# Where three weight chunks of the first expert are loaded: the later chunks' pool in place of the first chunks' buffers

## The chip, the core and the metric

The kernel runs on one core of one Trainium2 chip, in one launch. The metric is the device time of a run in microseconds. Every time below is of the kernel before the change.

## What is computed

Three stages follow each other. Sliding-window attention with sink tokens (2 batches, 8 heads, 768 positions, head width 64) gives 1536 rows of 512. A gated product follows, and then a mixture of eight experts: each token goes to one expert, in the order of the gate's logits over all tokens and experts, at most 192 tokens to an expert.

```python
x = attention(q, k, v, n_sink, window)          # (1536, 512)
x = (x @ w_a * (x @ w_b)) @ w_out               # w_a, w_b: 512 x 1536
logits = x @ w_gate                             # 8 experts
# greedy assignment in descending order of all logits, 192 tokens an expert
for e in range(8):
    out[mask[e]] = np.maximum(x[mask[e]] @ w1[e], 0.0) @ w2[e]   # 512 x 1024, 1024 x 512
```

## The kernel before, in words

All large products are made from split operands: a float32 operand is cut into a high part (`ehi`, `gh`, `woh`, ...) that TensorE (PE) takes at full rate and a low part (`elo`, `gl`, `wol`, ...) with the rest, and three products of the parts are added in PSUM.

*The second product and the routing* (`run`, from line 712). `second` computes x in twelve blocks of 128 tokens, 36 matmuls each (line 977). The routing's steps are woven into it by `fill`, so that PE has matmuls while DVE and ACT rank the logits. At the end of a block ACT copies it from PSUM (line 983), and ACT's DMA queue writes it to the tensor `x2d` in HBM (line 984). The last block, of 128 tokens, is also kept on the chip as `x2last`.

*The first expert's rows* (`first_rows`, line 1009). When the routing has given the tokens of each expert (`idx`), two indirect DMAs of POOL (GpSimd) gather the first expert's rows from the first eleven blocks of `x2d` into `first0` (128 rows) and `first1` (64 rows), line 1018. They have to wait until the eleventh block is written. Rows of the twelfth block don't come from HBM: a matmul with a 0/1 matrix picks them from `x2last` (line 1147). The gathered rows are turned by 16 matmuls with the identity (`begin_rows`, line 1035), eight for each gather.

*The weights of the experts.* Each expert has eight chunks of 512 KB, four of w1 and four of w2, so chunk c belongs to expert c // 8. `weight_load` (line 987) issues one DMA per chunk from SP's queue (line 997), into a buffer named `eraw`. ACT makes `ehi` from it (line 1002) and DVE `elo` (line 1007); then the buffer is free. Two pools hold `eraw`: `exraw` with three buffers (line 703), opened when the second product begins, and `more` with six buffers (line 1044), opened with the experts. Chunks 0 to 3 go to `exraw`, long before they are wanted; they are converted at the end of the routing (lines 738 to 743). SP's queue works strictly in order: a load whose buffer is not free holds up the loads behind it.

`more` lies in memory that the second product's operands and `x2` hold until then, so its first load waits for PE, ACT, POOL and the writes of x2d to be done with them.

*The experts* (`experts`, line 1038). PE, ACT and DVE work in the order in which the lines are written. For each expert, four steps make the hidden values (`product1`, line 1092; ACT's `part`, DVE's `h`, ACT's `hT`), then four steps make the output (`product2`, lines 1098 to 1103). In each step `high` converts chunks for later steps: the list CONV = (5, 6, 6, 7, 9, 10, 11, 12) says how many chunks of this expert and the next have to be converted by each of the eight steps. The conversion of chunk 4 stands in the first step, between `part` and `hT`. `load` (line 1072) is called for four chunks from the one being converted; SP runs ahead of this as far as free buffers let it. At the end of an expert's second step of outputs, the next expert's gathered rows (`xe`, line 1051) are turned.

Of the kernel before, what the change touches and what calls it, by code (L numbers as in the profile page):

```python
# [67 lines left out]
class Kernel:  # L68
# [969 lines left out]
    def experts(self, tag, exraw, trp, first=None, weights=None):  # L1038
# [4 lines left out]
        scat, xe, xt, raws, ready = [], {}, {}, {}, {}  # L1043
        with tc.tile_pool(name="ex" + tag, bufs=2) as pool, tc.tile_pool(name="er" + tag, bufs=EXR2) as more, \
# [26 lines left out]

            def load(c):
                if c < 8 * E and c not in raws and c not in ready:
                    raws[c] = self.weight_load(exraw if weights and c < 7 else more, c)

            def high(s):

                while pend:
                    self.weight_low(ready[pend.pop(0)])
                for c in range(8 * (s // 8) + CONV[s % 8]):  # L1080
                    if c < 8 * E and c not in ready:
                        for n in range(c, c + 1 + EARLY):
                            load(n)
                        ready[c] = self.weight_high(pool, raws.pop(c), EB)
                        pend.append(c)
# [47 lines left out]
            for c in range(4, 4 + EARLY):  # L1133
                load(c)
# [201 lines left out]
```

## Time and profile before

| | |
|---|---|
| Median of three runs | 646.68 us (645.85, 646.68, 648.88) |
| The profiled execution | 648.35 us, of which the span from the first to the last instruction is 646.1 us |
| PE busy | 620.3 us, 96% of the span |
| DVE, ACT, POOL busy | 404.0, 337.3 and 175.9 us (63%, 52%, 27%) |
| Mean granted clock of PE | 0.976 of full speed |
| DMA | 72.16 MB, 112 GB/s over the span |

The page divides the span into 40 slices of 16.2 us. PE is busy for 90% or more in nearly all of them, and the granted clock is below 90% in three: the first, the last, and the one from 468 to 485 us, where the second product has ended and the first expert begins. This is the place that the diff touches. In the rows below, times are microseconds from the start of the span; an entry "[7.54 <-DMA first]" says how long the engine was idle before the instruction and what ended that. Which event ended a wait is inferred from the times of the semaphore events, so of two events that fall together the wrong one can be named. PEld is the loading of weights into PE; an engine's name with a q behind it is its queue of instructions.

### The profile page before, as it was taken

Reading aid. Unit: us, or ns where it says so; the run is one execution under the profiler, and the core shown is the slowest. Engines: PE = TensorE matmul, PEld = TensorE weight load, DVE = VectorE, ACT = ScalarE, POOL = GpSimd, SP = SyncE. Lnnn points to the kernel's source line nnn. Section 1 sums busy time; section 2 is a strip of 40 time slices with the busy share of each in tenths; the row PEclk is TensorE's granted clock in tenths of the full one; section 3 lists DMA queues with packets and bytes.
Section 4 is the critical chain, followed back from the end, with each engine's and each line's share of the span. In section 5 each row is a group of like instructions: output and inputs, shape, how many; then the busy total and the mean of one; then the engine's idle time right before and its main releaser. Section 6 shows DMA issues by size and latency. Waiting matters only on the chain.

```text
span 646.1 us, 10265 instructions
## 1 busy us (share of the span) xinstructions
PE 620.3 (96%) x3705; PEld 491.2 (76%) x3705; DVE 404.0 (63%) x873; ACT 337.3 (52%) x669; POOL 175.9 (27%) x299
## 2 busy tenths in 40 slices
PE   7999999999999999999999999999869999999994
PEld 5767777778878888788866776677668888888883
DVE  5788876579966767342126556666207787777782
ACT  3788777644442334122126655663307666668671
POOL 5557664400000000001024344344321222232221
PEclk7999999999999999999999999999959999999997
DMA  7966310044542233200040000000381888787841
GB/s 161 219 123 159 66 67 2 2 129 133 164 130 77 88 98 98 66 0 1 0 131 17 18 33 17 34 17 33 119 281 26 276 253 260 257 245 231 259 144 34
DMA packets 82602, 72.16 MB, mean 112 GB/s; under 512 B 41072, under 2 KB 69744, under 8 KB 82544
## 3 DMA queue, kind: packets, MB, share of 16 engines
q1 hardware_dynamic: 78704, 61.99, 33.3%
q0 software_dynamic: 2112, 6.30, 3.0%
q10 hardware_dynamic: 1728, 3.15, 1.3%
q8 instruction: 31, 0.51, 0.3%
q14 instruction: 27, 0.22, 0.1%
HBM read 65.13 MB, written 6.29 MB: 111 GB/s over the span
## 4 chain that ended last, share of the span: by engine, by line
PE 80%; issue 9%; DVE 3%; DMA 2%; POOL 2%; ACT 1%; POOLq 0%; DVEq 0%; ACTq 0%
PE pa L559 14%; PE pb L559 14%; PE px L977 13%; PE p L1092 7%; PE pa L470 4%; PE s L273 4%; PE px L367 4%; PE pa L334 3%; POOL out_dram L1107 2%; PE pq L856 2%; PE pw L662 1%; PE pt L237 1%; DVE gt L845 1%; PE y L1098 1%; PE y L1099 1%
## 5 line engine op out<-in xcount | busy, mean ns | idle before, releaser
L1007 DVE TENSOR_TENSOR elo<-eraw,ehi 128x1024 fp32r<-128x1024 f32 x64 | 75.9, 1216 | 5.0 <-ACT ehi L1002 5.0
L1092 PE MATMUL p<-xt,ehi 128*128 128x384 f32 x256 | 73.6, 360 | 0.0
L963 POOL TENSOR_TENSOR gl<-G,gh 128x512 fp32r<-128x512 f32 (+1 forms) x40 | 47.9, 1206 | 71.5 <-ACT gh L962 71.5
L1002 ACT ACTIVATE ehi<-eraw 128x1024 fp32r<-128x1024 f32 x64 | 65.0, 1054 | 3.8 <-DVE oidx L932 2.3
L1092 PE MATMUL p<-xt,elo 128*128 128x192 f32 x256 | 64.7, 254 | 0.0
L977 PE MATMUL px<-woh,gh 128*128 128x512 f32 x144 | 59.9, 416 | 0.0
L279 ACT ACTIVATE A<-sm,negmax 128x264 f32<-128x264 f32 (+1 forms) x96 | 46.9, 490 | 23.6 <-DVE negmax L277 22.5
L963 POOL TENSOR_TENSOR gl<-GE,gh 128x256 fp32r<-128x256 f32 x8 | 7.1, 882 | 188.4 <-ACT gh L962 184.9
L845 DVE TENSOR_SCALAR gt<-lgT,vmax 128x1536 bf16<-128x1536 f32 x40 | 45.4, 1196 | 20.4 <-ACT lgT L820 17.7
L977 PE MATMUL px<-woh,gl 128*128 128x512 f32 x144 | 57.6, 400 | 0.0
L977 PE MATMUL px<-wol,gh 128*128 128x512 f32 x144 | 57.5, 399 | 0.0
L566 DVE TENSOR_TENSOR G<-asb,pb 128x512 f32<-128x512 f32 x32 | 21.9, 685 | 54.7 <-PE pb L559 54.7
L301 POOL TENSOR_SCALAR A<-A,rs 128x256 f32<-128x256 f32 (+1 forms) x96 | 43.2, 469 | 44.8 <-DVE rs L288 24.9
L559 PE MATMUL pb<-xh,whi 128*128 128x512 f32 x128 | 51.1, 399 | 0.0
L559 PE MATMUL pa<-xh,whi 128*128 128x512 f32 x128 | 50.9, 398 | 0.0
L1107 POOL DMA_INDIRECT out_dram<-o,oidx x16 | 26.3, 1645 | 90.2 <-ACT o L1116 68.2
L559 PE MATMUL pb<-xh,wlo 128*128 128x512 f32 x128 | 50.1, 391 | 0.0
L559 PE MATMUL pb<-xl,whi 128*128 128x512 f32 x128 | 50.0, 390 | 0.0
L559 PE MATMUL pa<-xh,wlo 128*128 128x512 f32 x128 | 49.9, 390 | 0.0
L1092 PEld LDWEIGHTS p<-xt,elo 128*128 128x128 f32 x256 | 49.4, 193 | 0.6 <-ACT xt L1069 0.2
L559 PE MATMUL pa<-xl,whi 128*128 128x512 f32 x128 | 49.8, 389 | 0.0
L1092 PEld LDWEIGHTS p<-xt,ehi 128*128 128x128 f32 x256 | 48.3, 189 | 0.7
(220 smaller groups left out, 1439.5 us busy)
## 6 DMA issues: line engine op xcount, KB each, us to landing
eraw<-in_moe_w_dram SPq DMA_DIRECT2D x64, 512.0 KB
wraw<-in_moe_w_a_dram SPq DMA_DIRECT2D x12, 512.0 KB
wraw<-in_moe_w_b_dram SPq DMA_DIRECT2D x12, 512.0 KB
wraw<-in_moe_w_out_dram SPq DMA_DIRECT2D x12, 512.0 KB
x2d<-x ACTq DMA_DIRECT2D x11, 256.0 KB
rawv<-in_v_dram SPq DMA_DIRECT2D x10, 256.0 KB
rawq<-in_q_dram SPq DMA_DIRECT2D x8, 256.0 KB
rawk<-in_k_dram SPq DMA_DIRECT2D x8, 256.0 KB
```

Source lines behind the costliest of these rows:

```text
L273: nc.tensor.matmul(s[:, :n], T[hs, tq, 6 + i % 2, 0:128], flat[hs, tk, lo:lo + n], start=(t == 0), stop=(t == 2))
L279: nc.scalar.activation(st.A2[:, j, h, c0:], sm[:, :n], AF.Exp, bias=self.negmax[:, cc], scale=-1.0, accum_out=self.sums[:, cc])
L301: nc.gpsimd.tensor_scalar(blocks, blocks, st.r2[:, j, h:h + 1], 1.0, op0=OP.mult, op1=OP.mult)
L367: nc.tensor.matmul(px[64 * h:64 * h + 64, cols], vv[:, vcol[h]], st.AT[h][:, sl].rearrange("p a b -> p (a b)"), start=(not g and n == 0), ...
L559: nc.tensor.matmul(pab[m], w[:, k, :], x[:, k, :], start=(k == 0 and t == 0), stop=(k == 3 and t == 2))
L845: nc.vector.tensor_scalar(gt, vrow, v, None, op0=OP.is_lt)
L963: nc.gpsimd.tensor_tensor(gl[:, fs], src, f32(gh[:, fs]), op=OP.subtract)
L977: nc.tensor.matmul(out[t], w[:, ff, :], x[f], start=(f == 0 and n == 0), stop=(f == 11 and n == 2))
L1002: self.nc.scalar.activation(hi, raw, AF.Copy)
L1007: (eng or self.nc.vector).tensor_tensor(lo, raw, f32(hi), op=OP.subtract)
L1092: nc.tensor.matmul(p1[:, ff, 0:c], w[:, k, cols], x[:, k, 0:c], start=(n == 0), stop=(k == 3), skip_group_check=True)
L1107: st = nc.gpsimd.indirect_dma_start(out=self.out, out_offset=bass.IndirectOffsetOnAxis(ap=self.oidx[:n, 2 * e + h:2 * e + h + 1], axis=0), ...
```

## The change

Chunks 0 to 3 stay in `exraw`. Chunks 4, 5 and 6 go to `more` instead of the three buffers that chunks 1, 2 and 3 leave. `weights` is the list of the four chunks that are converted ahead, so the bound falls from 7 to 4.

```diff
             def load(c):
                 if c < 8 * E and c not in raws and c not in ready:
-                    raws[c] = self.weight_load(exraw if weights and c < 7 else more, c)
+                    raws[c] = self.weight_load(exraw if weights and c < len(weights) else more, c)
```

SP's queue, behind the four loads of the first chunks and the reading of a flag (line 1197), holds the loads of chunks 4 to 15 in these rows (2x512 is a chunk of w2, 4x256 one of w1). The names in brackets are the counters that a load waits for: DMAHW0 to 7 are those of earlier transfers, the others are raised by DVE, PE, ACT and POOL. A row without brackets has nothing of its own to wait for.

```order
 L1197 ISA x2
-L997 DMA eraw<-in_moe_w_dram 128x2x512 [waits DMAHW6_49,DMAHW3_49,DVE_49]
-L997 DMA eraw<-in_moe_w_dram 128x2x512 [waits DMAHW7_49,DMAHW4_49,DVE_49]
-L997 DMA eraw<-in_moe_w_dram 128x2x512 [waits DMAHW6_49,DMAHW0_49,DVE_49]
-L997 DMA eraw<-in_moe_w_dram 128x2x512 [waits DMAHW1_49,DMAHW2_49,DMAHW0_49,DMAHW5_49,PE_49,DMAHW7_49,Activation_49,Pool_49]
+L997 DMA eraw<-in_moe_w_dram 128x2x512 [waits DMAHW3_49,DMAHW2_49,DMAHW4_49,DMAHW1_49,DMAHW5_49,DMAHW0_49,DMAHW6_49,PE_49,DMAHW7_49,Activation_49,Pool_49]
+L997 DMA eraw<-in_moe_w_dram 128x2x512 x3
 L997 DMA eraw<-in_moe_w_dram 128x4x256 x2
-L997 DMA eraw<-in_moe_w_dram 128x4x256 [waits DMAHW3_49]
-L997 DMA eraw<-in_moe_w_dram 128x4x256 [waits DMAHW4_49]
```

Before, the first three loads wait for DVE, that is for `elo` of chunks 1 to 3, and the fourth, chunk 7, for PE, ACT, POOL and the writes of x2d. Now chunk 4 has the fourth one's list, and chunks 5 to 9 follow it with nothing more to wait for; chunk 10 is the first that waits for DVE and ACT to give back a buffer of `more`, where it was chunk 13. The order of the instructions on PE, ACT, DVE, POOL and SP is the same in all that is executed.

## Rows read from the trace of the kernel before

**Rows 1.** Waits of PE: line and what it waited for, total us, times, longest.

```profile
PE pt L1035 <- DMA first<-x2d,idx: 7.5, 1, 7.5
PE pq L856 <- DVE gt L845: 2.2, 3, 0.8
```

**Rows 2.** Timeline of PE at the turn to the experts: start, us, instruction.

```profile
466.35 0.40 PE L977 MATMUL px<-woh,gl 128*128 128x512 f32 x1
474.30 3.97 PE L1035 MATMUL pt<-ident,first 128*128 128x128 f32 x16 [7.54 <-DMA first<-x2d,idx]
```

**Rows 3.** Windows: stretch, its length, PE busy (instructions), granted clock, DMA share, GB/s.

```profile
8.00:18.20 10.20, 9.82 (x50) 0.50 0.84 188
...
45.00:49.00 4.00, 2.74 (x25) 1.00 0.30 87
...
468.80:474.20 5.40, 0.00 (x0) 0.50 1.05 342
474.30:482.40 8.10, 8.10 (x30) 0.50 1.02 323
```

**Rows 4.** Chain of waits, 456 to 482 us: start, us, what.

```profile
461.98 5.07 DMA eraw<-in_moe_w_dram
467.04 7.21 DMA first<-x2d,idx
```

**Rows 5.** POOL's queue at line 1018, 465 to 467.5: waits passed, from first to last.

```profile
L1018 POOLq EVENT_SEMAPHORE  x3: 43/43/43, 466.0 to 466.2; - x3
```

**Rows 6.** Timeline of ACT's queue: the writes of x2d's tenth and eleventh block.

```profile
449.97 0.33 ACTq L984 DMA_DIRECT2D x2d<-x  x1
...
461.34 0.33 ACTq L984 DMA_DIRECT2D x2d<-x  x1
```

**Rows 7.** DMA engines, 449.9 to 453.9 in 40 slices of 0.1 us: busy tenths.

```profile
DMA  0000000008989997100000000000000000000000
```

**Rows 8.** Timeline of SP's queue: the loads of chunks 4 to 6, then chunk 7.

```profile
459.70 2.64 SPq L997 DMA_DIRECT2D eraw<-in_moe_w_dram  x3
...
466.89 0.37 SPq L997 DMA_DIRECT2D eraw<-in_moe_w_dram  x1
```

**Rows 9.** Queues (q1 SP, q10 ACT): packets, MB; 461.3 to 463.4, then 465.3 to 466.1.

```profile
q1 hardware_dynamic: 290, 0.56, 88.4%
q10 hardware_dynamic: 20, 0.04, 5.0%
...
q10 hardware_dynamic: 4, 0.01, 2.0%
```

**Rows 10.** Timeline of POOL: its last subtraction, and the second gather.

```profile
460.91 2.19 POOL L963 TENSOR_TENSOR gl<-G,gh 128x512 fp32r<-128x512 f32 x1 [4.49 <-ACT gh L962]
...
468.50 0.97 POOL L1018 DMA_INDIRECT first<-x2d,idx  x1 [0.30 <-issue]
```

**Rows 11.** The ten gathers into xe from 480 us on: issue to landing.

```profile
DMA to landing us min/median/max: 3.0/3.3/4.2
```

**Rows 12.** Timeline of ACT in the first expert.

```profile
481.16 0.49 ACT L1069 ACTIVATE xt<-pt 128x384 fp32r<-128x384 f32 x1 [0.73 <-PE pt L1147]
...
484.59 1.05 ACT L1002 ACTIVATE ehi<-eraw 128x1024 fp32r<-128x1024 f32 x1
...
497.18 2.96 ACT L1002 ACTIVATE ehi<-eraw 128x1024 fp32r<-128x1024 f32 x3
```

**Rows 13.** SP's queue, 466.9 to 471.1 and to 474; DMA busy tenths, 466.9 to 485.

```profile
q1 hardware_dynamic: 358, 0.61, 50.1%
...
q1 hardware_dynamic: 1012, 1.27, 58.5%
...
DMA  0035898999999999999999999999999984001000
```

**Rows 14.** Windows: experts two to eight; PE, PEld, DVE, ACT, POOL, clock, DMA, GB/s.

```profile
501.50:639.00 137.50, 135.43 (x777) 116.92 (x775) 102.03 (x158) 88.93 (x136) 33.91 (x24) 1.00 0.72 227
```

**Rows 15.** Waits of SP's queue: total us, times, longest.

```profile
SPq L997 <- DVE elo L1007: 130.0, 55, 27.0
```

## Prediction

> **What bounds the kernel now.** TensorE (PE) is busy for 96% of the span (table above), so only a place where PE stands still can give time back. The waits of PE name one such place: 7.5 us in one piece, at the 16 matmuls that turn the first expert's gathered rows (`first`, line 1035), for the DMA that brings those rows. Of the other waits behind the start of the run, none is longer than 0.8 us [rows 1]. PE's timeline shows it: the last matmul of the second product ends at 466.75, the next one starts at 474.30 [rows 2]. Behind it the clock is gone as well: from 468.8 to 482.4 the granted clock is 0.50, the lower of its two levels (1.2 instead of 2.4 GHz), and 8.1 us of PE work run at that level [rows 3]; in the experts behind it is 1.00 again [rows 14].
>
> Why do the rows come so late? The chain of waits says: a weight load (5.07 us), then the gather (7.21 us) [rows 4]. The first of these names needs correcting. POOL passes its waits for the gather at 466.0 and starts it at 467.04 [rows 4, 5]; what the gather reads is x2d, and the last block of x2d that it needs is written by the ACT queue's DMA of 461.34 [rows 6], while none of its waits is for one of the loads. So that write landed at 466.0, 4.7 us after its issue. The same write one block earlier, issued at 449.97, had the DMA engines to itself and moved between 450.8 and 451.6 [rows 6, 7]. The write of 461.34 shares them with the loads of chunks 4, 5 and 6, which SP issues from 459.70 to 462.34 [rows 8]: between 461.3 and 463.4 the weights' queue moved 290 packets, 0.56 MB, and the write 20, or 0.04 of its 0.26 MB [rows 9]. It is these three loads that the change takes away from there.
>
> **The change, step by step.** (1) *Three loads start later.* They have the buffers of chunks 1 to 3 now, free when DVE is done with each. In the pool of the later chunks they lie where the second product's tiles were, and the first of them takes over the wait of today's chunk 7, which passes at 466.89 [rows 8], once PE's last matmul is over. No instruction is added, and none changes its place on PE, ACT, DVE, POOL or SP in what is executed.
>
> (2) *The write lands earlier.* Alone, its packets were through 1.6 us after the issue [rows 6, 7]. From the last packets to POOL's release lie at most 0.7 us: the contended write still has 4 packets after 465.3 [rows 9]. So it lands 1.6 to 2.3 us after issue; I take 2.1, that is at 463.45 instead of 466.0. POOL's own work before the gather ends at 463.10 [rows 10], just in time. The Trainium skill (DMA: Bandwidth & Descriptors, section Queues, rings and completion order) says that each DMA engine takes turns between the queues that have work, a packet at a time. By that rule the loads would merely have doubled the write's moving time of 0.8 us, removing them would give 0.8 us instead of 2.55, and the sum below would be 8.0 instead of 9.8 us; 20 packets against 290 is no such sharing, and I go by the row.
>
> (3) *The gather starts and lands earlier.* From release to gather POOL needs 1.0 us (466.03 to 467.04 today) [rows 4, 5], so it starts at 464.45. Today it lands after 7.2 us, because six more loads and the last x2d block start at 466.9 to 470 and fill the engines. The ten gathers issued from 480 on, of the same two sizes, land in 3.0 to 4.2 us, 3.3 in the middle [rows 11]. I take 3.3, since now no load is issued before 466.89 and the rows should be there at 467.75. The bounds are 3.0 and 7.2. PE then waits from 466.75 to 467.75: 1.0 us instead of 7.54, a gain of **6.5 us**. The second gather follows 1.46 us behind the first (468.50 today [rows 10]), at 465.9, and lands near 469.0; PE is through the first eight matmuls about 1.0 us after it began (half of 3.97 us [rows 2], at twice the clock), so it waits **0.2 us** more there.
>
> (4) *The clock stays up.* The 8.1 us at 0.50 hold about 1.05 us in which PE waits for ACT's copy (0.49 us [rows 12]) and DVE's subtraction behind it, and those do not follow PE's clock. The other 7 us halve: a gain of **3.5 us**, at most 4.05. Is a stop of 1.0 us short enough? Between 45 and 49 us PE was busy for 2.74 of 4.0 us, so it stood still for 1.26, and the granted clock remained 1.00 [rows 3]. That is the nearest row, and I take it; the case in which it falls all the same is a rival below.
>
> (5) *Are the weights there when they are wanted?* ACT works in a fixed order: behind the first expert's first `part` it converts chunk 4, and if that has not landed, `hT`, the next products and all the rest stand behind it. ACT reaches it at 484.59 today [rows 12], at 474.8 then. Chunk 4 takes the place of the load that is first at 466.89 today: by 471.1 its queue had moved 0.61 MB, one chunk is 0.52 MB [rows 13], so it has 3.7 us to spare. By 474 it had moved 1.27 MB [rows 13], so chunk 5 is there before ACT begins with chunk 4. All six loads, the x2d block and six gathers were through by 483 [rows 13]; chunk 9, the first of the three conversions at 497.18 today [rows 12], is wanted at 487.4 then. So this costs nothing, and the cover is 3.7 us at its thinnest. From chunk 10 on each load waits for the buffer six chunks back, as every load from chunk 13 on does today.
>
> Sum: -6.5 + 0.2 - 3.5 = **-9.8 us**. The profiled execution took 648.35 us, so it would take 638.6. It stands 1.7 us above the median of the runs shown (646.68); for the median I forecast 646.7 - 9.8 = 636.9, rounded **637.0 us**.
>
> **The rivals.**
>
> *The clock falls nevertheless (641.6 us).* The new stop is followed by transposes and by short waits for ACT and DVE, not by dense matmuls. At the start of the run the clock, once down, stayed at 0.50 from 8.0 to 18.2 us [rows 3]. Should it fall at about 468.8 and stay down so long, 10.2 us run at half speed: 5.1 us lost at most, some 4.6 without the waits for ACT and DVE. For it: that row, where PE was not idle either while the clock stayed low, and behind the start of the run no stop as long as 1.0 us in one piece shows the clock kept. Against it: the row at 45 us, with more idle time in all.
>
> *The gather stays slow (644.1 us).* If its 7.2 us are its own and not the other traffic's, it lands at 471.65, PE waits 4.9 us, and the clock falls as today: a gain of 2.6 us, which is less than a measurement of this kernel can tell from no change (0.5%, 3.2 us). Against it stand the ten gathers at 3.0 to 4.2 us; for it, that this is the first gather of the run.
>
> *No change (646.7 us).* The loads start as late as planned, but the write takes its 4.7 us for a reason of its own, or another wait of the gather ends at 466. The write of 449.97 speaks against it.
>
> *Slower: the stream of weights becomes the bound (650.9 us).* Today nine chunks can lie ready ahead of the first expert's second product, then only six, since the three old buffers stay empty. Seven experts take 137.5 us [rows 14], 19.6 each, 2.45 us per chunk. In the crowd of 466.9 to 483 the six loads took 16.1 us, 2.7 each [rows 13]. Should the loads run at that pace throughout, ACT would wait 0.25 us per chunk, 14 us over the 56 chunks of seven experts; less the 9.8 gained that is 4.2 us more than today. It decides from 2.45 us per chunk on. Against it: SP waits 130 us in all for free buffers [rows 15], so today the loads wait for room and not the reverse, with the DMA engines busy 0.72 of that stretch [rows 14]. The Trainium skill (Trainium Kernel Development and Optimization, section Best Practices) asks for DMA to be overlapped with compute; the change does the opposite for 1.5 MB, which now start when the second product is over. By that rule it loses; the rows say that what the loads lay beside was a write that PE waits for.
>
> **How the numbers follow.** Forecast 0.63; the clock falls 0.20; slow gather 0.08; no change 0.04; slower 0.05. The forecast's own bounds: the write's landing (0.5 us earlier, 0.2 later), the gather's 3.0 to 4.2 us, the clock's 4.05 us, and the spread of the runs (0.8 below their median, 2.2 above). That gives some 635 to 640 us. The range reaches from 635.0 to 643.5 to hold the second case with its spread. Faster by over 0.5% are the first two cases, 0.83; within 0.5% the next two, 0.12; slower 0.05.
>
> **What would show it.** Right: SP's first load after the flag is read at about 466.9 and not at 459.7; POOL's first gather near 464.5; the wait of PE at line 1035 about 1 us; the granted clock 1.00 throughout 468 to 482; `ehi` of chunk 4 with no wait for a DMA. Step 2 is wrong if the gather still starts near 467, step 3 if it starts early and lands later than 469, step 4 if the clock is 0.50 behind a short stop, step 5 if ACT waits for `eraw`. The forecast as a whole is wrong if the median is above 643.5.

## The result, and the profile after

| | before | after |
|---|---|---|
| median of the runs shown, us | 646.99 (645.85 to 648.88, 4 runs) | 640.47 (639.09 to 643.18, 4 runs) |
| ratio of the times | 1 | 0.9893 (95%: 0.9865 to 0.9921) |
| profiled execution, us | 648.35 | 643.18 |
| its span, us | 646.1 | 641.1 |

The change makes the kernel 6.5 us faster (1.1%). The forecast was 637.0 us, in a range from 635.0 to 643.5: right in its direction, and 3.5 us too low. The 640.5 us lie outside the 635 to 640 that the forecast gave to its own case, and inside the range because that was widened to hold the case in which the clock falls.

The two profiled executions don't begin alike: the first row below answers to the row at 8 us of [rows 3]. The first stretch at half clock lasts from 8 to 24 us here and from 8 to 18 us there, and the last px matmul starts at 468.72 instead of 466.35. That is no doing of the change: in a second execution of the changed kernel (below) that matmul starts at 467.56. So the stage is measured from that matmul on.

The waits of PE, the kernel after:

```profile
PE pt L1035 <- DMA first<-x2d,idx: 2.4, 2, 1.3
```

The wait of 7.5 us [rows 1] has become two, 2.4 us together. PE's timeline at the same place as [rows 2], kernel after:

```profile
468.72 0.40 PE L977 MATMUL px<-woh,gl 128*128 128x512 f32 x1
470.47 1.16 PE L1035 MATMUL pt<-ident,first 128*128 128x128 f32 x8 [1.34 <-DMA first<-x2d,idx]
472.67 1.10 PE L1035 MATMUL pt<-ident,first 64*128 64x64 f32 x8 [1.04 <-DMA first<-x2d,idx]
486.00 0.41 PE L1098 MATMUL y<-ehi,hT 128*128 128x512 f32 x1
```

PE stops 1.34 us for the first gather and 1.04 us for the second; the kernel before stopped once, and both gathers were there afterwards. From the last px to the first y the stage takes 17.28 us (486.00 - 468.72). In the kernel before that y starts at 490.88:

```profile
490.88 0.41 PE L1098 MATMUL y<-ehi,hT 128*128 128x512 f32 x1
```

So the stage was 490.88 - 466.35 = 24.53 us, and 7.25 us are gained in it, where the forecast had 9.8. Less the 2.4 us of the later start, that is, to 0.1 us, the 5.0 us by which the spans differ.

The chain of waits, kernel after (start, us, what), beside [rows 4]:

```profile
459.76 0.81 ACT ehi L1002
...
460.73 1.99 ACT ehi L1002 x2
462.72 0.52 ACT gh L962
463.24 0.49 ACT x L983
463.75 2.02 DMA x2d<-x
...
466.85 1.16 POOL first L1018
468.01 0.30 issue
468.31 4.31 DMA first<-x2d,idx
```

No weight load stands in it now. The write of x2d's block is itself the link, 2.02 us from issue to landing. Ahead of it stands something that the wrong link of [rows 4] had hidden: ACT converts chunks 1 to 3 before it copies the block. SP's first load starts at 469.26, behind the last px, as foreseen:

```profile
469.26 0.88 SPq L997 DMA_DIRECT2D eraw<-in_moe_w_dram  x2
```

The windows (columns as in [rows 14]), kernel after: first the start, then the stage.

```profile
8.00:24.20 16.20, 15.66 (x82) 11.88 (x82) 8.83 (x40) 8.92 (x31) 5.85 (x20) 0.50 0.99 202
...
468.80:474.80 6.00, 3.62 (x25) 3.04 (x24) 0.00 (x0) 0.68 (x2) 0.48 (x1) 1.00 0.92 286
474.90:478.20 3.30, 3.30 (x13) 2.98 (x12) 1.11 (x2) 0.79 (x2) 1.97 (x3) 0.50 1.06 395
478.30:484.00 5.70, 5.70 (x42) 5.70 (x41) 3.05 (x6) 3.74 (x7) 1.69 (x2) 1.00 0.88 265
494.00:632.00 138.00, 138.00 (x787) 118.78 (x785) 104.67 (x161) 89.58 (x137) 32.94 (x23) 1.00 0.73 228
```

PE is busy for 3.62 of 6.00 us, and behind that the clock is at its lower level for 3.3 us, while PE is already at work without a pause. In the kernel before it was low for 13.6 us [rows 3], of which 5.4 lay inside the stop, where PE had nothing to do. The experts run at 1.00 and PE is busy throughout; from the first y to the end of the span it is 155.2 us before and 155.1 us after. So the weights' stream costs nothing.

### The profile page after: what moved, and what is told of

Same layout as the page of the kernel before. It is cut to its first block, busy times and chain, and to the rows that moved or that the text cites. A ratio compares the mean times of both kernels' runs of the same rounds, so it can differ in the third digit from the quotient of the medians.

```text
span 641.1 us, 10268 instructions
## 1 busy us (share of the span) xinstructions
PE 621.2 (97%) x3705; PEld 491.7 (77%) x3705; DVE 404.0 (63%) x873; ACT 337.5 (53%) x669; POOL 176.0 (27%) x299
## 4 chain that ended last, share of the span: by engine, by line
PE 81%; issue 9%; DVE 3%; POOL 2%; DMA 2%; ACT 1%; POOLq 0%; DVEq 0%; ACTq 0%
PE pa L559 14%; PE pb L559 14%; PE px L977 13%; PE p L1092 7%; PE s L273 4%; PE pa L470 4%; PE px L367 4%; PE pa L334 3%; POOL out_dram L1107 2%; PE pq L856 2%; PE pt L237 2%; PE pw L662 1%; DVE gt L845 1%; PE y L1098 1%; PE y L1099 1%
## 5 line engine op out<-in xcount | busy, mean ns | idle before, releaser
L845 DVE TENSOR_SCALAR gt<-lgT,vmax 128x1536 bf16<-128x1536 f32 x40 | 45.4, 1197 | 20.4 <-ACT lgT L820 17.7
```

The lines of the kernel that those rows point to most:

```text
L845: nc.vector.tensor_scalar(gt, vrow, v, None, op0=OP.is_lt)
```

## The experiments

The kernel before stood at 648.3 to 648.8 us on the chips of these runs, a little above the 647.0 of the result, so the times are compared by their ratios. The table has the readings; the sections say what follows from each. "Write to gather" is from the issue of the x2d block's write on ACT's queue to POOL's start of the first gather; "stage" is from the last px matmul to the first y, both from the timelines. "At half clock" is the stretch at 0.50 from the first of these stops on; where PE stands for 7 us and more it begins inside the stop, 5.4 us before its end in the kernel before and some 3 us in the two like it.

| kernel | loads beside the write | write to gather, us | stops of PE, us | at half clock, us | stage, us | ratio to before (95%) |
|---|---|---|---|---|---|---|
| before | 3 | 5.70 | 7.54 | 13.6 | 24.53 | 1 |
| after | 0 | 3.10 | 1.34, 1.04 | 3.3 | 17.28 | 0.9893 (0.9865 to 0.9921) |
| after, again | 0 | 3.10 | 1.23, 1.01 | 6.6 | 18.69 | 0.9883 (0.9847 to 0.9919) |
| one early | 1 | 3.56 | 1.73, 2.23 | 6.7 | 20.31 | 0.9914 (0.9884 to 0.9944) |
| two early | 2 | 5.76 | 7.75 | 10.1 | 24.62 | 0.9984 (0.9962 to 1.0005) |
| three unused loads | 3 | 5.84 | 8.15 | 10.2 | 25.01 | 1.0 (0.9975 to 1.0026) |
| before, filled | 3 | 5.51 | 0.40 | none | 21.25 | 0.9936 (0.9919 to 0.9953) |
| after, filled | 0 | 3.12 | 0.41 | none | 15.67 | 0.987 (0.9849 to 0.989) |
| late loads | 0 | 3.11 | 1.27, 0.20 (for xt) | none | 15.00 | 0.9854 (0.9833 to 0.9875) |
| copy first | 0 | 3.11 | 1.09, 0.55 (for xt) | none | 14.89 | 0.984 (0.9823 to 0.9857) |
| copy first, one | 0 | 3.09 | 0.55 (for xt) | none | 13.88 | 0.9829 (0.9805 to 0.9853) |

### The change again

> The changed kernel once more, for a profile that can be laid beside the three that follow and for a tighter ratio. Theory (the gather starts when the x2d block's write has landed, and the write is late only where weights are being read beside it): the same picture as in its first profile, about 640.5 us, 6.5 below the kernel before: two stops of PE at the pt matmuls (L1035), together 2.4 us where the kernel before has one of 7.54, and a stretch of 3 to 4 us at half clock after them where the kernel before has 13.7. Rival (the first profile's 641.1 with its late start was a freak): the stops or the half clock are gone or several us longer in this one.

The picture is the same: stops of 1.23 and 1.01 us. The stretch at half clock is not, it is twice as long:

```profile
471.80:478.40 6.60, 6.60 (x24) 6.25 (x24) 1.12 (x2) 0.98 (x2) 3.20 (x4) 0.50 1.06 384
```

With nearly equal stops the stage is 18.69 us here and 17.28 there. The gain in the stage is thus 5.8 to 7.3 us, and the length of the half clock varies between executions of one and the same kernel.

### Loads back beside the write: one, two, and three whose data nothing uses

One, and two:

```diff
-raws[c] = self.weight_load(exraw if weights and c < len(weights) else more, c)
+raws[c] = self.weight_load(exraw if weights and c < len(weights) + 1 else more, c)
```

```diff
-raws[c] = self.weight_load(exraw if weights and c < len(weights) else more, c)
+raws[c] = self.weight_load(exraw if weights and c < len(weights) + 2 else more, c)
```

Three, ahead of the loads of chunks 4 to 6, which stay in the later pool:

```diff
             if not weights:
                 high(0)
+            if weights:
+                for c in range(4, 7):
+                    self.weight_load(exraw, c)
             for c in range(4, 4 + EARLY):
                 load(c)
```

> Chunk 4 alone goes back to the buffers of the first four, so one load of 0.5 MB instead of three is under way beside the x2d block's write. Theory (it is the bytes read beside the write that delay it): the write lands between the 2.0 us of the changed kernel and the 4.7 us of the kernel before, about 3 us after its issue; the gather starts about 1 us later than in the changed kernel and PE stands 3 to 4 us in all: 641.5 to 643.5 us. Rival A (it is how many loads stand in the queue, not their bytes, or any load at all): the write takes 4.7 us again and the time is 646 to 647. Rival B (what the change brought came from chunk 4 to 6's own place in the later pool, not from the write): the write's time does not matter, and 640.5 or better since chunk 4 is there earlier.

> Chunks 4 and 5 go back to the buffers of the first four: two loads beside the write. Theory (bytes beside the write): the write lands about 4 us after its issue, PE stands 5 to 6 us, 643.5 to 645.5 us, between one load and the three of the kernel before. Rival A (any load at all): 646 to 647, as with one load. Rival B (the chunks' place in the pool): no worse than the changed kernel, 640.5.

> The changed kernel with three more loads of 0.5 MB into the old buffers, whose data nothing uses, at the point where the kernel before had those of chunks 4 to 6; the chunks themselves stay in the later pool. Theory (only the reads beside the write matter): the write lands 4.5 to 5 us after its issue again, PE stands 7 to 8 us, the clock is halved for more than 10 us, and the time is that of the kernel before or a little above it, 646 to 648 us. Rival (where the chunks lie, or which wait their loads have, is what counts): the time stays at 640 to 641 us.

With three unused loads the time is that of the kernel before, ratio 1.0, although the chunks lie where the change puts them. So the place of the chunks, and the wait that their loads have, are worth nothing; what is read beside the write is worth all of the gain. One load costs little (0.9914, its interval overlaps the change's own). Two cost as much as three, and here the expectation of something in between failed. The chains show how. First one early load, then two:

```profile
462.52 2.44 DMA x2d<-x
...
466.08 1.16 POOL first L1018
467.24 0.30 issue
467.54 5.46 DMA first<-x2d,idx
```

```profile
461.31 4.72 DMA x2d<-x
...
467.07 7.33 DMA first<-x2d,idx
```

With one load the write lands in 2.44 us, with two in 4.72. The queues in the 2.1 us behind the write's issue (q1 is SP's, q10 ACT's; packets, MB, share) show what passed first; one early load, then two, then three unused:

```profile
q1 hardware_dynamic: 220, 0.42, 51.9%
q10 hardware_dynamic: 144, 0.26, 32.0%
```

```profile
q1 hardware_dynamic: 271, 0.52, 77.7%
q10 hardware_dynamic: 29, 0.06, 7.2%
```

```profile
q1 hardware_dynamic: 264, 0.51, 80.1%
q10 hardware_dynamic: 2, 0.00, 0.5%
```

The single load was issued 1.6 us ahead of the write (460.88), and once it was through, the write had room for all of its 144 packets in that time. With two loads SP is at issuing until just ahead of the write (461.17 against 461.31), with three until 1.0 us behind it, as in the kernel before [rows 6, 8], and in that time the write moves 0.06 MB or nothing. That is not the whole of the delay: in the kernel before, the write's packets move from 462.8 to 465.8, 3.0 us, where alone they take 0.8 us, and in this stretch loads move beside them. From 463.4 to 464.6 SP's queue moves 88 packets and ACT's 86. So the write begins 0.7 us later behind its issue than alone (1.5 us instead of 0.8) and loses the rest, some 2 us, by sharing the engines with the later loads.

The second half of the loss is the gather. It takes 7.3 us with two loads and 7.2 in the kernel before [rows 4], though by then the early loads are through. What it meets are, by the rows below, the loads that start when PE is done with px, at 466.83 with two loads and 466.89 before [rows 8]:

```profile
466.83 3.15 SPq L997 DMA_DIRECT2D eraw<-in_moe_w_dram  x5
```

The first gathers start at 467.07 and 467.04, just behind these. In the changed kernel the two gathers start 2.4 us (466.85 against 469.26) and 0.95 us (468.31) ahead of them. The queues of the kernel before from 466.9 to 471.9 show the order:

```profile
q1 hardware_dynamic: 654, 0.92, 59.1%
q10 hardware_dynamic: 144, 0.26, 14.0%
```

In these 5 us the loads and the last block's write move, and the gathers' own queue (q0) nothing; in the kernel after, 92 packets of q0 are through 3.6 us behind the first gather's start. So a write that is 2.7 us late puts the gather behind the next loads, and by these rows that costs it some 3.6 us more (7.2 against 3.62 from the gather's start to PE's in the kernel after). No run holds the later loads back in the kernel before, so this part rests on the traces.

### The clock alone: PE's stop filled

The kernel before, with matmuls whose product nothing uses in the place of the stop:

```diff
+                junk = rpsum.tile([128, 4, 128], F32, name="junk", tag="pv", bufs=2)
+                onesb = self.rc[1]
+                for _ in range(33):
+                    nc.tensor.matmul(junk, onesb, onesb.unsqueeze(1).to_broadcast([128, 4, 128]), start=True, stop=True)
                 for h in range(2):
                     for k in range(4):
                         self.begin_rows(pts[k // 2][:, k % 2, :], rows, h, k)
```

and the changed kernel with `range(8)` in the same lines.

> The kernel before, its loads and its late gather untouched, with 33 matmuls of 128x512 in bf16, whose product nothing uses, on PE between the last px matmul and the pt matmuls: at some 0.21 us each they take the 7.5 us in which PE stood. This prices the clock alone. Theory (the stop is what lets the clock fall, and the fall costs time of its own): the half clock from 468.8 to 482.4 is gone, the gather's delay stays, and the kernel is 2.5 to 4.5 us faster than before, ratio 0.993 to 0.996. Rival A (the clock falls here whatever PE does): no change, or slower by some tenths where the matmuls run past the gather. Rival B (the half clock is hidden beside the waits for xt and ehi): the clock stays up and the time stays too, ratio 1.0.

> The changed kernel with 8 such matmuls, about 1.7 us, at the same place: they cover the first of the two stops (1.2 to 1.3 us), and the second gather, at 4.2 us, still ends the second. Theory (the short half clock that is left, 3.4 to 6.8 us in the two profiles of the changed kernel, comes from the stops): the clock stays up or is down for 3.4 us at most, and the time is 0.5 to 2.5 us below the changed kernel's, 0.984 to 0.988 of before. Rival A (the clock falls because of the second stop or of what PE does behind it): half clock as before, 0.988 to 0.990. Rival B: the added matmuls delay the pt matmuls, and it is up to 1 us slower than the changed kernel.

PE's timeline and the windows of the kernel before, filled:

```profile
465.56 7.30 PE L749 MATMUL junk<-onesb 128*128 128x512 bf16 x33
473.26 2.19 PE L1039 MATMUL pt<-ident,first 128*128 128x128 f32 x16 [0.40 <-DMA first<-x2d,idx]
```

```profile
465.40:472.80 7.40, 7.40 (x35) 3.12 (x33) 0.00 (x0) 0.60 (x1) 3.09 (x3) 1.00 0.81 256
472.90:482.40 9.50, 9.01 (x59) 8.37 (x60) 2.29 (x5) 3.04 (x6) 2.70 (x3) 1.00 0.94 285
```

The gather comes as late as ever, PE does nothing useful meanwhile, and yet the kernel is 0.64% faster (3.0 to 5.3 us by the interval): the clock is 1.00 where it was 0.50 [rows 3], and the same 16 transposes take 2.19 us instead of 3.97 [rows 2]. The stage falls by 3.28 us. This is the price of the clock in the kernel before, forecast at 3.5.

In the changed kernel eight such matmuls cover the first stop. The second shrinks to 0.41 us, the clock stays at 1.00, and the stage falls to 15.67 us, from 17.28 and 18.69. So the short half clock came from the stops. Of the 1.6 and 3.0 us, 0.5 and 0.35 are the rows of the second gather, which are there sooner (3.44 us behind the start of the last px, instead of 3.95 and 3.79); the rest, 1 to 2.7 us, is what the clock cost. By the total times alone the difference (0.987 against 0.9893 and 0.9883) lies within the intervals.

### Later loads held back until the gathers have landed

A one-element copy by ACT from the second gather's tile into the raw tile, ahead of each of the six loads of chunks 4 to 9:

```diff
-    def weight_load(self, pool, c):
+    def weight_load(self, pool, c, late=None):
...
         raw = pool.tile([128] + shape, F32, name="eraw", tag="eraw")
+        if late is not None:
+            self.nc.scalar.activation(raw[0:1, 0, 0:1], late[0:1, 0:1], AF.Copy)
...
+            for c in range(4, 4 + EXR2 if weights else 4):
+                raws[c] = self.weight_load(more, c, first[0][1][0])
```

> The changed kernel with the loads of chunks 4 to 9 held back until both gathers have landed (a one-element copy by ACT from the second gather's tile into each of the six raw tiles ahead of its load). This takes away what the second gather shares the queues with. Theory (the second gather took 4.2 to 4.3 us and the first 3.6 because loads and the last block's write ran beside it): the second gather lands in about 3.2 us, the second stop of PE falls from 1.0 us to 0.2 or nothing, and the chunks, 3 us later, are still there when ACT wants chunk 4: 1 to 2.5 us below the changed kernel, 0.984 to 0.987 of before. Rival A (the second gather is slow by itself, behind the first on POOL's queue): the stop stays at 1 us and the time at 0.988. Rival B (the later chunks become the bound): a wait for eraw before chunk 4's or 5's conversion and 1 to 3 us slower than the changed kernel.

The timelines of POOL, PE and ACT, in this order, with the loads held back:

```profile
464.52 1.16 POOL L1020 DMA_INDIRECT first<-x2d,idx  x1 [1.35 <-issue]
465.98 0.97 POOL L1020 DMA_INDIRECT first<-x2d,idx  x1 [0.30 <-issue]
```

```profile
468.06 2.19 PE L1037 MATMUL pt<-ident,first 128*128 128x128 f32 x16 [1.27 <-DMA first<-x2d,idx]
```

```profile
469.00 0.67 ACT L993 ACTIVATE eraw<-first 1x1 f32<-1x1 f32 x6 [1.57 <-DMA first<-x2d,idx]
```

ACT's copies wait for the second gather alone: it has landed at 469.0, 3.0 us after its issue at 465.98, instead of 4.3. PE's second stop is gone, the 16 transposes run in one piece. The first stop is as long as in the changed kernel, 1.27 us, and yet the clock stays up:

```profile
466.40:468.00 1.60, 0.39 (x2) 0.00 (x0) 0.00 (x0) 0.60 (x1) 0.55 (x1) 1.00 0.61 187
468.10:474.80 6.70, 6.50 (x43) 5.92 (x43) 1.12 (x2) 1.74 (x9) 3.48 (x4) 1.00 0.77 251
```

The stage is 15.00 us, 9.5 us less than before, and the ratio 0.9854 is 9.5 us of 648.3: nearly the 9.8 of the forecast. By the total times the gain over the changed kernel lies within the intervals; the stage shows it, 2.3 to 3.7 us shorter. The loads start at 469.23, 2.8 us behind the last px, and no conversion of the first expert waits for one. So rival A (the second gather slow by itself) and rival B (late chunks) both fall.

### ACT's copy of the block ahead of the conversions

The chain of the kernel after names ACT's three conversions (2.8 us) ahead of the block's copy. Here they, and DVE's parts of them, move behind the copy of the last block; a one-column copy keeps them there in ACT's order:

```diff
-                    weights.append(self.weight_high(pre2 if c else pre, self.weight_load(exraw, c), 3 if c else 1))
-                    self.weight_low(weights[c])
+                    raw = self.weight_load(exraw, c)
+                    weights.append((pre2, raw) if c else self.weight_high(pre, raw, 1))
+                self.weight_low(weights[0])
...
+            if weights:
+                mark = pool.tile([128, 1], F32, name="mark", tag="mark")
+                nc.scalar.activation(mark, first[1][:, 0:1], AF.Copy)
...
-                ready[c] = w
+                ready[c] = self.weight_high(w[0], w[1], 3) if c else w
...
                         for j in range(2):
                             split(0, j, pts[j])
+                        if weights:
+                            for c in (1, 2, 3):
+                                self.weight_low(ready[c])
```

> The changed kernel with ACT's conversions (ehi) of chunks 1 to 3, and DVE's elo of the same chunks, moved behind ACT's copy of the last block: ACT's copy of block 10, which stood 2.5 us behind those conversions in the changed kernel, follows PE's product at once. Theory (the write's issue is now set by ACT's order, and what follows it is write 2.0 us, POOL 1.1 us, gather 3.6 and 4.2 us): the write is issued some 2.5 us earlier, both gathers have landed when PE is through with the last px matmul or 0.5 us later, PE hardly stops, the clock stays up, and the time is 3 to 5 us below the changed kernel's, 0.980 to 0.984 of before. Rival A (POOL's own gl, not the write, sets the gather's start then): 1 us of it is left over, 0.984 to 0.987. Rival B (the conversions behind the copy make xt or chunk 1 late): a stop of PE at the p matmuls takes the place of those at pt, 0.988 or slower.

The wait for the gather is gone altogether, and so is the half clock. Another wait, a shorter one, has taken its place, as rival B had it, but the sum is a gain. It is for xt, the turned rows, which ACT copies from pt and DVE splits. PE's timeline:

```profile
464.89 2.09 PE L1036 MATMUL pt<-ident,first 128*128 128x128 f32 x16
466.91 1.57 PE L1151 MATMUL pt<-ones,x2last 128*128 128x192 f32 x8
469.56 0.47 PE L1093 MATMUL p<-xt,elo 128*128 128x192 f32 x2 [1.09 <-ACT xt L1070]
470.58 0.45 PE L1093 MATMUL p<-xt,ehi 128*128 128x384 f32 x1 [0.55 <-DVE xt L1071]
```

On ACT the three conversions, 2.9 us, stand ahead of xt. So two more kernels leave two of them, or one, there and put the rest behind xt; with one (in the other, 2 and 3 change places with 1, 2 and 3 accordingly):

```diff
-                ready[c] = self.weight_high(w[0], w[1], 3) if c else w
+                ready[c] = self.weight_high(w[0], w[1], 3) if c == 1 else w
...
                         if weights:
+                            for c in (2, 3):
+                                ready[c] = self.weight_high(*ready[c], 3)
                             for c in (1, 2, 3):
                                 self.weight_low(ready[c])
```

> The version with ACT's copy of block 10 ahead of the conversions, in which PE now stands 1.1 + 0.5 us at the p matmuls because xt waits behind three ehi conversions (2.9 us) on ACT: here ehi of chunk 3 goes behind xt, so that two conversions (1.9 us) stand between the last block's copy and xt. Theory (the gathers are out of the way, and ACT's order is the only cause of what is left): the stop before the p matmuls falls by about 1 us, the stage from the last px matmul to the first y from 14.9 to about 14 us, and the time by 0.5 to 1.2 us: 0.982 to 0.984 of before. Rival (chunk 3's conversion comes late for its p matmuls, or stands before the part copy of chunk 0 instead): a stop of the same size at a later p, and the time stays at 0.984.

> The same with ehi of chunks 2 and 3 behind xt, one conversion before it. Theory: the two conversions behind xt take 2 us of ACT while PE works off chunk 0's p matmuls (2.5 us), so it is as good as with one behind, 0.982 to 0.984. Rival: chunk 1's elo or the part copy of chunk 0 come late, and PE stands 0.5 to 1 us at a later p: 0.984 to 0.986.

> The version with three conversions behind the copy once more, on the same chip as the two others, since they differ by less than two chips may: 0.984 of before and the same two stops of 1.1 and 0.5 us.

With one conversion ahead the ratio is 0.9829 (0.9805 to 0.9853), with two 0.9836 (0.9813 to 0.986), with all three on the same chip 0.9851 (0.9825 to 0.9877). The intervals overlap, so the total times don't rank them. The stages do, 13.88, 14.09 and 15.04 us: the stop of 1.1 us before the p matmuls is gone in the first two, and no later one has come. ACT with one conversion ahead of xt:

```profile
468.25 1.04 ACT L1003 ACTIVATE ehi<-eraw 128x1024 fp32r<-128x1024 f32 x1
469.90 0.49 ACT L1070 ACTIVATE xt<-pt 128x384 fp32r<-128x384 f32 x1 [0.61 <-PE pt L1151]
470.55 0.49 ACT L1070 ACTIVATE xt<-pt 128x384 fp32r<-128x384 f32 x1 [0.16 <-PE pt L1151]
470.94 2.00 ACT L1003 ACTIVATE ehi<-eraw 128x1024 fp32r<-128x1024 f32 x2
```

xt now waits for PE and not for ACT's own queue. This version is 9.5 to 12.7 us faster than the kernel before, and its stage is 3.4 to 4.8 us shorter than the changed kernel's.

## Why the forecast was right, and where it was off

*Step 1, three loads start later: right.* SP's first load is at 469.26, 0.54 us behind the start of the last px, as chunk 7's was before (466.89 against 466.35).

*Step 2, the write lands earlier: right.* Forecast 2.1 us from the issue, measured 2.02. The unused loads show that this is what the change is worth: with them the time is that of before. The Trainium skill (DMA: Bandwidth & Descriptors, section Queues, rings and completion order) has the engines take turns between queues, by which, as the forecast read it, the write would have been only 0.8 us late. It was 2.7 us late. But the row of 20 packets against 290, by which the forecast set the rule aside, ends before the two queues had worked side by side for long: from 463.4 to 464.6 they moved 86 and 88 packets, and there the trace agrees with the rule. So what the rows contradict is the 0.8 us, and not that the queues take turns.

*Step 3, the gather starts and lands earlier: right for the first, mis-sized for the second.* The step put the second gather's landing near 469.0, 3.1 us behind its start, with 0.2 us of waiting (with the 3.3 us that it took for the first gather it would have been 469.2 and some 0.45 us). That is the time of a gather alone, although by its own step 1 the loads start while the second is under way. The second gather took 4.31 us and the stop was 1.04 us. With the loads held back it took 3.0 us and there was no stop. The first gather's stop was 1.34 us instead of 1.0 (3.62 us from its start to PE's, not 3.3). Together that is 1.2 us of the 2.55 us that the stage fell short of 9.8 in the first profile (7.25), and 1.0 us of 3.96 in the second (5.84). The 6.5 us between the medians lie between the two.

*Step 4, the clock stays up: this step failed, though its price was right.* It had the clock at 1.00 throughout, behind one stop of 1.0 us and one of 0.2. With the loads held back, one stop of 1.27 us did leave the clock at 1.00. What came in the changed kernel was two stops of 1 us and more, with PE busy for 3.62 of 6.00 us, and then the clock was down for 3.3 us, in the second profile for 6.6. At half clock a stretch loses at most half of its length, 1.65 or 3.3 us, and that is room for the rest of the shortfall, 1.4 and 2.9 us. The full price, 3.5 us by the forecast, was 3.28 us in the stage and 0.64% of the time (4.1 us, 3.0 to 5.3) when PE's stop was filled. With the loads held back the second stop and the half clock went together, so one error, the second gather, cost twice: once as a stop and once by the clock. That is one execution with a profile; how long the clock is down differs between executions of one kernel, and why is not shown.

*Step 5, the weights are there: right.* ACT's conversion of chunk 4 starts at 479.70 straight behind `part`:

```profile
479.31 0.49 ACT L1160 ACTIVATE part<-p 128x384 f32<-128x384 f32 x1 [3.26 <-PE p L1092]
479.70 1.05 ACT L1002 ACTIVATE ehi<-eraw 128x1024 fp32r<-128x1024 f32 x1
```

*The rivals.* "The clock falls nevertheless" (641.6 us) is nearest in time, but the case is a milder one: the clock fell later and for 3 to 7 us, not 10.2, and a quarter to a half of the shortfall is the stops themselves. "The gather stays slow" fell with 3.6 us, and "no change" with the write's 2.02. "The stream of weights becomes the bound" fell twice: PE is busy for all of 494 to 632 us, and even with the loads held back 2.3 us more nothing waits for them. So the rule of the Trainium skill (Trainium Kernel Development and Optimization, section Best Practices) that DMA be overlapped with compute did not decide here: 1.5 MB less beside the second product cost nothing.

Not tried: the write on another queue than ACT's, and ACT's new order with the loads in their old buffers. Why the write's packets took 3.0 us beside the later loads, and not twice their 0.8 us, is not settled either.

## What to carry to other kernels

Look at what small transfers a prefetch passes on its way: a load with room to spare can delay a write that someone waits for, and the wait then stands at a gather far from both. Where a late transfer slips behind the next batch of loads, it loses twice; hold those back, or issue the small one first. Price a stop of PE together with the slower clock behind it, and trace the chain again after the fix: the next link here (ACT's conversions ahead of the copy) was worth a further 3 to 5 us in the stage.

## What the runs showed of the hardware that was not expected

- A write of 0.26 MB landed in 2.0 us alone, 2.44 us beside one load of 0.5 MB issued 1.6 us ahead of it, 4.7 us beside two and also beside three: a step and not a slope. Beside the one load its packets came behind the load's; beside three they moved together with those of the later loads, 86 and 88 in 1.2 us.
- One stop of 1.27 us left the clock at 1.00, two of 1.2 and 1.0 us brought it to 0.50, for 3.3 us in one execution of the kernel and for 6.6 us in another. In these two it fell when PE was at work again; in the kernel before, 2 us into the stop of 7.5 us, and beside two loads 4 us into one of 7.75.
- The gather of 64 rows took 3.0 us with no loads beside it and 4.3 us where they started 1 us behind it. The gather of 128 rows took 3.5 us with none, 3.6 us where they started 2.4 us behind it, and 7.2 to 7.7 us where they started just ahead of it.
